# The order of the four last parts of a W4 product: alternating between two PSUM pairs

## The chip, the cores and the metric

The kernel runs on one core of one Trainium2 chip. The metric is the device time of one execution in microseconds. Most executions of a kernel agree within 0.3%. That is about 0.8 us here.

In views of the profile, PE is TensorE's matmul, PEld its weight load, DVE is VectorE, ACT is ScalarE, POOL is GpSimd and SPq the queue that issues the stores. PSUM is the memory that TensorE's matmuls write and VectorE reads. The slot of a matmul is the time from its start to the next one's start in an unbroken stream; a stall between slots is what such a step takes beyond its slot. L484 is line 484 of the kernel.

## The reference, cut to what matters

A gated sum of a linear-attention block and a mixer block, on 2048 rows of width 640. The end of the second block is what the change touches:

```python
x1 = x + hs                                         # [2048, 640]
h2 = gelu(layernorm(x1) @ w3) @ w4                  # w3: 640 x 1728, w4: 1728 x 640
b  = x1 + h2
return g * a + (1 - g) * b
```

## The kernel before

The rows go through in four tiles of 512, each of four chunks of 128 rows. `W4` is the last product of a tile, so in the last tile it is the last thing TensorE does. Its 1728 contraction rows are 13 full blocks of 128 and a rest of 64.

In the cuts below, `P` is 128, `D` 640, `TS` 512, `LT` 256, `NT` the four tiles, `FF` the 13 full blocks, and `cc` the number of a chunk in its tile.

PSUM is handed out in pairs of banks, four pairs in all:

```python
ps = ctx.enter_context(tc.tile_pool(name="ps", bufs=4, space=PSUM))
def pair():
    return ps.tile([P, 2, 512], F32, name="pp")
```

In the last tile, each odd chunk (1 and 3) is cut into a small part of 128 output columns (`hf == 0`), in bank 0 of its pair, and a big part of 512 columns (`hf == 1`), in bank 1:

```python
def w4_dst(t, cc, pts, hf):
    n = D - TS if t == NT - 1 and cc % 2 else LT        # D - TS = 128, LT = 256
    return (pts[cc][:, 0, TS - n:TS], 0, n) if hf == 0 else (pts[cc][:, 1, 0:D - n], n, D)

def w4_mm(t, cc, pts, hf, start):                       # 13 matmuls
    dst, a, b = w4_dst(t, cc, pts, hf)
    for fc in range(FF):
        nc.tensor.matmul(dst, lhsT=st[t]["h2"][:, fc * TS + cc * P:fc * TS + (cc + 1) * P],
                         rhs=w4_sb[:, fc, a:b], start=start and fc == 0, stop=not start and fc == FF - 1)

def w4_part(t, cc, pts, hf):                            # VectorE reads one part, then it is stored
    # ... (cut)
    nc.vector.scalar_tensor_tensor(oc[:, a:b], src, omg[:, c:c + 1], st[t]["x1"][cc][:, a:b],
                                   op0=ALU.mult, op1=ALU.add)
    nc.sync.dma_start(out2[c * P:(c + 1) * P, a:b], oc[:, a:b])

def w4_tile(t):
    # ... the even chunks' 52 matmuls, and pairs for chunks 1 and 3 (cut)
    w4_rest(t, pts)                                     # the rest of 64 rows, for all chunks
    # ... (cut)
    for cc in (0, 2):
        w4_out(t, cc, pts[cc])                          # VectorE reads the even chunks, stores them
    last = t == NT - 1
    for cc, hf in ((3, 1), (1, 1), (1, 0), (3, 0)) if last else ((1, 0), (1, 1), (3, 0), (3, 1)):
        # ... (cut)
        w4_mm(t, cc, pts, hf, False)
        if last:
            w4_part(t, cc, pts, hf)
        elif hf == 1:
            w4_out(t, cc, pts[cc])
```

So the last tile ends with four parts on TensorE: big 3, big 1, small 1, small 3. Each is read by VectorE as soon as it is done.

## Time and profile before

| | before |
|---|---|
| median of the three fast runs | 266.64 us |
| span of the profiled run | 264.5 us |
| TensorE busy, granted clock | 98%, 1.000 |
| TensorE idle, waiting for VectorE, in the last tile | 0.84 us |

Of the page of before, the busy table and the two lines of the chain that ended last:

```profile
PE 260.0 (98%) x1744; PEld 161.5 (61%) x1744; DVE 139.5 (53%) x271; ACT 85.2 (32%) x126; POOL 21.9 (8%) x67
...
PE 97%; ACT 1%; DVE 0%; issue 0%
PE pp L484 22%; PE pp L464 21%; PE pp L311 8%; PE pp L194 8%; PE pp L417 8%; PE pp L448 8%; PE pp L345 8%; PE pp L236 8%; PE pp L206 1%; PE pp L472 1%; PE pp L493 1%; ACT m_sb L385 1%; PE pp L364 1%; PE pp L251 0%; DVE oc L512 0%; PE pp L383 0%
```

TensorE bounds the kernel from end to end. Only a hole in TensorE's work, its start, or the tail after its last matmul, can be shortened without less work. The timeline of before shows one such hole at the end. Its columns are start and length in us, engine, line, operation, and in brackets the idle time before it and what ended it:

```profile
253.52 5.79 PE L484 MATMUL pp<-w_sb,h 128*128 128x512 bf16 x26
256.54 0.75 DVE L512 SCALAR_TENSOR_TENSOR oc<-pp,omg,x 128x512 bf16<-128x512 f32 x1 [1.51 <-PE pp L484]
...
259.34 0.75 DVE L512 SCALAR_TENSOR_TENSOR oc<-pp,omg,x 128x512 bf16<-128x512 f32 x1 [2.05 <-PE pp L484]
260.15 1.61 PE L484 MATMUL pp<-w_sb,h 128*128 128x128 bf16 x26 [0.84 <-DVE oc L512]
...
261.07 0.35 DVE L512 SCALAR_TENSOR_TENSOR oc<-pp,omg,x 128x128 bf16<-128x128 f32 x1 [0.98 <-PE pp L484]
261.80 0.35 DVE L512 SCALAR_TENSOR_TENSOR oc<-pp,omg,x 128x128 bf16<-128x128 f32 x1 [0.38 <-PE pp L484]
```

Read it so. The two big parts run without a gap (26 matmuls). VectorE reads big 3 at 256.54 while TensorE works on big 1: nobody waits. VectorE reads big 1 at 259.34, and TensorE stands still until that read is over. The reason put forward is that its next part, small 1, lies in the same pair. Then both small parts run (26 matmuls, one group). The view of waits from 240 us on names the hole (who waited for whom: us in total, times, longest):

```profile
PE pp L484 <- DVE oc L512: 0.8, 1, 0.8
```

And the chain in order of time (start, us, what) shows that the hole is on the path that sets the end:

```profile
253.59 5.73 PE pp L484 x26
259.32 0.02 issue
259.34 0.76 DVE oc L512
260.11 0.04 issue
260.15 1.62 PE pp L484 x26
261.77 0.03 issue
261.80 0.35 DVE oc L512
```

### The profile page before, as it was taken

Reading aid. Unit: us, or ns where it says so; the run is one execution under the profiler, and the core shown is the slowest. Engines: PE = TensorE matmul, PEld = TensorE weight load, DVE = VectorE, ACT = ScalarE, POOL = GpSimd, SP = SyncE. Lnnn points to the kernel's source line nnn. Section 1 sums busy time; section 2 is a strip of 40 time slices with the busy share of each in tenths; the row PEclk is TensorE's granted clock in tenths of the full one; section 3 lists DMA queues with packets and bytes.
Section 4 is the critical chain, followed back from the end, with each engine's and each line's share of the span. In section 5 each row is a group of like instructions: output and inputs, shape, how many; then the busy total and the mean of one; then the engine's idle time right before and its main releaser. Section 6 shows DMA issues by size and latency. Waiting matters only on the chain.

```text
span 264.5 us, 4272 instructions
## 1 busy us (share of the span) xinstructions
PE 260.0 (98%) x1744; PEld 161.5 (61%) x1744; DVE 139.5 (53%) x271; ACT 85.2 (32%) x126; POOL 21.9 (8%) x67
## 2 busy tenths in 40 slices
PE   8999999999999999999999999999999999999994
PEld 5767555788755644555667555667565667455743
DVE  1788688899858588955403464503455313112132
ACT  1555444321165636622502212312131422233000
POOL 7100220012300140001000001000001000000000
PEclk9999999999999999999999999999999999999999
DMA  7999987055663727600132000042000041100011
GB/s 203 181 209 367 376 255 287 0 42 121 127 91 71 78 51 196 203 0 2 25 74 77 25 0 2 0 99 77 25 0 2 1 99 58 43 0 2 0 50 50
DMA packets 46285, 23.62 MB, mean 89 GB/s; under 512 B 35770, under 2 KB 45626, under 8 KB 46266
## 3 DMA queue, kind: packets, MB, share of 16 engines
q1 hardware_dynamic: 45824, 22.86, 34.7%
q10 hardware_dynamic: 442, 0.49, 0.5%
q8 instruction: 13, 0.21, 0.3%
q14 instruction: 6, 0.05, 0.1%
HBM read 12.21 MB, written 2.62 MB: 56 GB/s over the span
## 4 chain that ended last, share of the span: by engine, by line
PE 97%; ACT 1%; DVE 0%; issue 0%
PE pp L484 22%; PE pp L464 21%; PE pp L311 8%; PE pp L194 8%; PE pp L417 8%; PE pp L448 8%; PE pp L345 8%; PE pp L236 8%; PE pp L206 1%; PE pp L472 1%; PE pp L493 1%; ACT m_sb L385 1%; PE pp L364 1%; PE pp L251 0%; DVE oc L512 0%; PE pp L383 0%
## 5 line engine op out<-in xcount | busy, mean ns | idle before, releaser
L464 PE MATMUL pp<-lnxT,w_sb 128*128 128x512 bf16 x260 | 60.4, 379 | 0.0
L484 PE MATMUL pp<-w_sb,h 128*128 128x256 bf16 (+3 forms) x416 | 58.0, 299 | 0.8 <-DVE oc L512 0.8
L466 ACT ACTIVATE h<-pp 128x1024 bf16<-128x1024 f32 (+1 forms) x28 | 27.0, 963 | 82.1 <-PE pp L464 82.1
L484 PEld LDWEIGHTS <-h 128*128 128x128 bf16 x416 | 39.3, 98 | 18.8 <-issue 2.2
L464 PEld LDWEIGHTS <-w_sb 128*128 128x128 bf16 x260 | 25.4, 98 | 26.8
L500 DVE SCALAR_TENSOR_TENSOR oc<-pp,omg,x 128x640 bf16<-128x640 f32 x14 | 12.0, 881 | 41.4 <-ACT h2x L475 21.3
L451 DVE SCALAR_TENSOR_TENSOR x<-pp,gate,x 128x640 f32<-128x640 f32 x16 | 13.9, 868 | 29.4 <-PE pp L448 29.4
L420 DVE TENSOR_TENSOR x<-pp,x_sb 128x640 f32<-128x640 f32 x16 | 13.1, 820 | 22.6 <-PE pp L417 22.6
L186 ACT ACTIVATE e<-pp 128x640 bf16<-128x640 f32 (+1 forms) x26 | 21.5, 827 | 9.6 <-PE pp L236 9.6
L448 PE MATMUL pp<-m_sb,pqT 128*128 128x320 bf16 x160 | 24.3, 299 | 0.0
L417 PE MATMUL pp<-w_sb,hsT 128*128 128x320 bf16 x160 | 23.9, 299 | 0.1
L194 PE MATMUL pp<-wk_sb,xT 128*128 128x320 bf16 (+1 forms) x160 | 22.6, 300 | 0.0
L311 PE MATMUL pp<-x_sb,pk 128*128 128x320 bf16 (+1 forms) x160 | 22.3, 300 | 0.0
L236 PE MATMUL pp<-xT,hsT 128*128 128x512 bf16 x100 | 21.7, 379 | 0.0
L311 PEld LDWEIGHTS <-pk 128*128 128x128 bf16 x160 | 18.8, 117 | 3.5
L417 PEld LDWEIGHTS <-hsT 128*128 128x128 bf16 x160 | 15.6, 98 | 8.2 <-issue 0.2
L448 PEld LDWEIGHTS <-pqT 128*128 128x128 bf16 x160 | 15.7, 98 | 7.7
L194 PEld LDWEIGHTS <-xT 128*128 128x128 bf16 x160 | 15.6, 98 | 6.2 <-DMA xT<-in_A_x_dram 0.3
L345 PE MATMUL pp<-lnxT,w_sb 128*128 128x512 bf16 x80 | 17.9, 379 | 0.0
L236 PEld LDWEIGHTS <-hsT 128*128 128x128 bf16 x100 | 11.8, 118 | 9.7
L281 POOL TENSOR_SCALAR rstd<-mv 128x4 f32<-128x4 f32 (+1 forms) x11 | 3.5, 314 | 156.4 <-DVE mv L287 156.4
L188 DVE SCALAR_TENSOR_TENSOR pk<-pp,e 128x640 bf16<-128x640 f32 x16 | 13.2, 825 | 1.7
(77 smaller groups left out, 194.8 us busy)
## 6 DMA issues: line engine op xcount, KB each, us to landing
out_dram<-oc SPq DMA_DIRECT2D x14, 160.0 KB, 1.8
w_sb<-in_B_w_dram SPq DMA_DIRECT2D x1, 2080.0 KB, 10.0
w_sb<-in_B_w_dram SPq DMA_DIRECT2D x1, 1296.0 KB, 8.0
x_sb<-in_A_x_dram SPq DMA_DIRECT2D x2, 640.0 KB, 10.4
x_sb<-in_A_x_dram SPq DMA_DIRECT2D x1, 1120.0 KB, 7.9
wo_sb<-in_A_wo_dram SPq DMA_DIRECT2D x6, 160.0 KB, 6.7
w_sb<-in_B_w_dram SPq DMA_DIRECT2D x1, 864.0 KB, 5.1
hsT<-in_A_wqkv_dram SPq DMA_DIRECT2D x1, 800.0 KB, 5.4
```

The source lines that it names most:

```text
L186: nc.scalar.activation(ev, src, ACT.Exp)
L188: nc.vector.scalar_tensor_tensor(dst, src, 0.0, ev, op0=ALU.max, op1=ALU.add)
L194: nc.tensor.matmul(pt[:, hf, 0:n], lhsT=xT[:, dc, c * P:(c + 1) * P], rhs=wk_sb[:, dc, hf * HD:hf * HD + n], start=(dc == 0), stop=(dc == ...
L236: nc.tensor.matmul(pt[:, t % 2, :], lhsT=wq_sb[:, dc, :].rearrange("p (m j) -> p j m", j=DC)[:, j], rhs=xT[:, dc, t * TS:(t + 1) * TS], st ...
L311: nc.tensor.matmul(pt[:, hf, 0:HD + hf], lhsT=w, rhs=x_sb[:, c, hf * HD:(hf + 1) * HD + hf], start=(c == 0), stop=(c == NCH - 1))
L345: nc.tensor.matmul(pt[:, i, :], lhsT=w, rhs=lnxT[t][:, dc, :], start=(dc == 0), stop=(dc == DC - 1))
L417: nc.tensor.matmul(pt[:, hf, 0:HD], lhsT=hsT[:, fc, 2 + c * P:2 + (c + 1) * P], rhs=w2_sb[:, fc, hf * HD:(hf + 1) * HD], start=(fc == 0), ...
L448: nc.tensor.matmul(pt[:, hf, 0:HD], lhsT=pqT[:, j, c * P:(c + 1) * P], rhs=m_sb[:, j, hf * HD:(hf + 1) * HD], start=(j == 0), stop=(j == D ...
L451: nc.vector.scalar_tensor_tensor(x1, pt[:, :, 0:HD], gate[:, c:c + 1], x1, op0=ALU.mult, op1=ALU.add)
L464: nc.tensor.matmul(pt[:, k, :], lhsT=w3_sb[:, dc, fc * P:(fc + 1) * P], rhs=lnT[:, dc, :], start=(dc == 0), stop=(dc == DC - 1))
L466: nc.scalar.activation(h2[:, 2 * i * TS:(2 * i + n) * TS], pt[:].rearrange("p h e -> p (h e)")[:, 0:n * TS], ACT.Gelu_apprx_tanh)
L484: nc.tensor.matmul(dst, lhsT=st[t]["h2"][:, fc * TS + cc * P:fc * TS + (cc + 1) * P], rhs=w4_sb[:, fc, a:b], start=start and fc == 0, stop ...
```

## The change

The intent: order the four parts so that a part never follows directly on one in its own pair. VectorE then reads one pair while TensorE writes the other.

```diff
         last = t == NT - 1
-        for cc, hf in ((3, 1), (1, 1), (1, 0), (3, 0)) if last else ((1, 0), (1, 1), (3, 0), (3, 1)):
+        for cc, hf in ((1, 1), (3, 1), (1, 0), (3, 0)) if last else ((1, 0), (1, 1), (3, 0), (3, 1)):
```

## The prediction

> **What bounds the kernel now.** TensorE. The busy table has PE at 260.0 of 264.5 us (98%); the chain that ended last is 97% PE; the per-core view shows the clock at 1.000. The stretch that the change touches is the last 11 us. The timeline there, with starts of single instructions (each odd chunk has a 512-column part in one bank of its PSUM pair, a 128-column part in the other):
>
> - big part of chunk 3: 13 matmuls from 253.52, 216 ns apart; VectorE reads it at 256.54 for 0.75 us;
> - big part of chunk 1: 13 matmuls, the last starting at 258.93; VectorE reads it from 259.34 to 260.10;
> - small part of chunk 1: it sits in the pair that VectorE is reading, and the build's wait is on the whole pair. PE is idle "0.84 <-DVE oc L512" (also the view of waits), and starts at 260.15;
> - small part of chunk 3: no wait. The 26 small matmuls start 55.7 ns apart, 260.15 to 261.54;
> - VectorE 261.80 to 262.15, DMA issue at 262.18, end at 264.5.
>
> **What the change removes, adds, moves.** No instruction is added or removed. The order becomes: big 1, big 3, small 1, small 3. Comparing the built programs, the first small matmul of chunk 1 keeps its wait on VectorE and that of chunk 3 gains one.
>
> Small 1 now needs only VectorE's read of big 1, over at about 257.3, long before PE gets there. So it follows big 3 directly: the next slot after the matmul at 258.93 is 259.14. It needs 13 x 55.7 ns = 0.725 us, until 259.87. Small 3 then waits for VectorE's read of big 3, in the same place as the read of before: released at 260.15. So PE's wait does not vanish. It shrinks from about 1.01 us between slots (258.93 + 0.216 to 260.15) to about 0.28 us. In the view of waits, which starts at the modelled end of a matmul, 0.84 us becomes about 0.1 us.
>
> **How much is critical.** All of it: in both kernels PE restarts at 260.15, with 26 matmuls left before and 13 after. PE's last matmul moves from 261.54 to about 260.82, by 0.725 us. Behind it nothing new queues: VectorE's read of small 1 (0.35 us) fits between 260.15 and 260.55, ahead of small 3's at about 261.08. The tail from PE's end to the span's end (2.7 us) stays. Expected span 263.7 us.
>
> **Trainium skill.** "PSUM — Partial Sum Buffer", section on bank collisions, asks for guarding by bank and quadrant. The two parts lie in different banks, so the wait of 0.84 us comes from tracking the pair as one tile; the change hides most of it and doesn't remove it. "Perfetto Trace Analysis", section on Tensor Engine instructions, says that the end of a matmul is estimated; hence I count from start to start.
>
> **Predicted time.** 266.78 - 0.73 = 266.05 us, range 265.5 to 266.6. Chances: faster by over 2%: 0.5%; within 2%: 99%; slower: 0.5%.
>
> **What would show it.** Right: PE's wait before the last small part is 0.05 to 0.3 us; no gap before small 1; the last VectorE instruction starts near 261.08. Wrong: a gap before small 1 too, or the last VectorE start still past 261.5.
>
> **What would make it wrong.** The gain is 0.3%, as large as the scatter between runs. A restart of PE after the wait slower than before; VectorE's read of small 1 going late and pushing the last one; the last stores landing later because they lie closer together.

## The result, and the profile after

The median was 265.77 us (265.64 to 265.81, 4 runs) against 266.71 us of before in the same rounds, or 266.64 us for its three fast runs. The ratio of the fast runs is 0.9965, with a 95% interval of 0.9945 to 0.9984. (Ratios are the mean time of one kernel's fast runs over that of the other's of the same rounds, so not quite the ratio of the medians that are quoted.) One run of before took 392.44 us; it is in the median of 266.71 us but was not counted as fast, and nothing here explains it.

The timeline after. The 52 matmuls of the four parts now come out as one group without an idle entry; the two VectorE reads, of big 3 and of small 1, are back to back and are merged:

```profile
253.80 7.51 PE L484 MATMUL pp<-w_sb,h 128*128 128x512 bf16 x52
...
256.82 0.75 DVE L512 SCALAR_TENSOR_TENSOR oc<-pp,omg,x 128x512 bf16<-128x512 f32 x1 [1.51 <-PE pp L484]
...
259.62 1.08 DVE L512 SCALAR_TENSOR_TENSOR oc<-pp,omg,x 128x512 bf16<-128x512 f32 x2 [2.05 <-PE pp L484]
...
261.35 0.35 DVE L512 SCALAR_TENSOR_TENSOR oc<-pp,omg,x 128x128 bf16<-128x128 f32 x1 [0.65 <-PE pp L484]
```

The chain in order of time, after:

```profile
253.87 5.73 PE pp L484 x26
259.60 0.02 issue
259.62 0.76 DVE oc L512
260.39 0.04 issue
260.43 0.90 PE pp L484 x13
261.33 0.02 issue
261.35 0.35 DVE oc L512
```

The chain still goes through VectorE's read of a big part, at the same 0.76 us. What differs is the piece behind it: 13 matmuls instead of 26. The other 13 (small 1) run beside the read. This is the whole change in two lines of a profile.

The view of waits after lists no wait of TensorE for VectorE at all. The costliest groups of the page still show 0.1 us of idle time before this group of TensorE (0.8 before):

```profile
L484 PE MATMUL pp<-w_sb,h 128*128 128x256 bf16 (+3 forms) x416 | 58.0, 299 | 0.1
```

For exact lengths we count single records from the start of the first big matmul. The Trainium skill, page "Perfetto Trace Analysis", section on Tensor Engine instructions, says that a matmul's end in the profile is estimated; its start is not, so the times run from start to start:

```
us from the first big matmul                  before    after
start of the last big matmul                   5.407    5.406
start of the first small matmul                6.629    5.622
start of the 13th small matmul                 7.295    6.292
start of the 14th (next part)                  7.351    6.628
start of the last matmul                       8.021    7.295
start of the last VectorE instruction          8.279    7.552
from there to the end of the trace             2.671    2.677
```

The gain in the last tile is 8.279 - 7.552 = 0.727 us, with the same tail behind it.

The two profiled spans differ by only 0.5 us, though (264.5 and 264.0). The rest lies at the other end of the kernel. In the chain in order of time, before (taken in two windows, the first of which cuts the length of its last piece, so only the starts count):

```profile
27.44 20.72 PE pp L236 x96
...
245.87 7.06 PE pp L484 x52
```

and after, in the same two windows:

```profile
27.72 20.29 PE pp L236 x94
...
246.16 7.06 PE pp L484 x52
```

After was already 0.28 us late at the start of the `q` products, and 0.29 us late at the start of the last W4 product. In the ten traces that kept all 1744 matmul records, the time from the 195th matmul to the first big matmul was 223.65 us, the same to 0.01 us, while the start of the first big matmul ran from 253.52 to 254.30 us. So the scatter between these traces is made in the first 30 us, long before the edited lines run. The single starts show two parts of it. From 4.8 to 5.8 us the 128x320 matmuls of after start some 267 ns apart, while those of before come every 136 ns from 5.2 us on; this makes after 0.46 us late. Why the faster pace comes later in some runs is not known. Then before, at 16.4 us, waits for the load of an input (`xT`) and loses 0.18 us of its lead. The same two parts differ in the other traces.

### The profile page after: what moved, and what is told of

Its sections match the earlier page's. It is cut to its first block, busy times and chain, and to the rows that moved or that the text cites. A ratio compares the mean times of both kernels' runs of the same rounds, so it can differ in the third digit from the quotient of the medians.

```text
span 264.0 us, 4272 instructions
## 1 busy us (share of the span) xinstructions
PE 260.3 (99%) x1744; PEld 161.8 (61%) x1744; DVE 139.5 (53%) x271; ACT 85.1 (32%) x126; POOL 21.9 (8%) x67
## 4 chain that ended last, share of the span: by engine, by line
PE 97%; ACT 1%; DVE 0%; issue 0%
PE pp L484 21%; PE pp L464 21%; PE pp L194 8%; PE pp L311 8%; PE pp L417 8%; PE pp L448 8%; PE pp L345 8%; PE pp L236 8%; PE pp L206 2%; PE pp L472 1%; PE pp L493 1%; ACT m_sb L385 1%; PE pp L364 1%; PE pp L251 0%; DVE oc L512 0%; PE pp L383 0%
```

## The experiments

The theory: TensorE's wait is decided by whether the next part lies in the pair that VectorE is reading. Alternating hides that read behind the small part put in between, so it saves the smaller of two lengths: the stall between slots (1.01 us here) and the small part (13 x 55.7 ns = 0.725 us). Alternation here means that a part is never followed by one of its own pair. Rivals: it matters which chunk goes first, or the order of VectorE's reads and of the stores; or the saving is the whole read, or a fixed amount.

The yardstick of all expectations is the time from the first big matmul to the start of the last VectorE instruction. The traces of two runs (e4, e5) lost the record of that matmul. There the yardstick is taken from an earlier anchor, the start of VectorE's last attention update, which is 8.617 us before the first big matmul in both before and after.

### The change itself again

No edit; five rounds.

> The changed kernel itself, to measure the gain with more rounds. Yardstick in the trace for all these runs: from the start of the first 512-column matmul of the odd chunks in the last tile to the start of the last VectorE instruction; before 8.28 us, after 7.55 us. Theory (the pair's wait is hidden behind the small part of chunk 1): 7.55 us again, and a timed gain of 0.73 us. Rival (the timed 0.94 us holds something besides this): a gain of 0.9 us or more that repeats.

Yardstick 7.551 us. Median 266.03 us against 266.42, ratio 0.998 (0.9967 to 0.9993), which is 0.5 us. A later repeat is told at the end. The 0.94 us of the first rounds did not repeat; 7.55 us did.

### Mirrored alternation

(The diffs from here on are shortened. This one and the next are shown against before.)

```diff
-((3, 1), (1, 1), (1, 0), (3, 0)) if last
+((3, 1), (1, 1), (3, 0), (1, 0)) if last
```

> Big 3, big 1, small 3, small 1: alternating like the change, but chunk 3 first, so the first half of the order of before is kept. Theory: yardstick 7.55 us and the same gain as the change, 0.73 us. Rival (it matters that chunk 1 goes first, or the order of the first two parts and of their stores): 8.28 us, no gain.

Yardstick 7.552 us; median 265.89 us, ratio 0.9977 (0.9964 to 0.9989). The first two parts keep the order of before and the gain is the same, so it is not chunk 1 going first.

### The big parts swapped, no alternation

```diff
-((3, 1), (1, 1), (1, 0), (3, 0)) if last
+((1, 1), (3, 1), (3, 0), (1, 0)) if last
```

> Big 1, big 3, small 3, small 1: the first half of the change with the small parts the other way round, so that the small part after the two big ones sits in the pair VectorE is reading. Theory: the whole wait is back, TensorE idle 0.84 us, yardstick 8.28 us, time as before within 0.1 us. Rival (the change's gain is that chunk 1's big part goes first): 7.55 us.

The wait is back whole. The timeline of this run:

```profile
259.73 0.75 DVE L512 SCALAR_TENSOR_TENSOR oc<-pp,omg,x 128x512 bf16<-128x512 f32 x1 [2.06 <-PE pp L484]
260.54 1.61 PE L484 MATMUL pp<-w_sb,h 128*128 128x128 bf16 x26 [0.84 <-DVE oc L512]
```

Yardstick 8.279 us; median 266.59 us, ratio 1.0006 (0.9994 to 1.0017).

### The order of before, the small parts in each other's pairs

```diff
     def w4_dst(t, cc, pts, hf):
         n = D - TS if t == NT - 1 and cc % 2 else LT
-        return (pts[cc][:, 0, TS - n:TS], 0, n) if hf == 0 else (pts[cc][:, 1, 0:D - n], n, D)
+        home = pts[4 - cc] if t == NT - 1 and cc % 2 and hf == 0 else pts[cc]
+        return (home[:, 0, TS - n:TS], 0, n) if hf == 0 else (home[:, 1, 0:D - n], n, D)
```

> The order of before on every engine and in the stores, but each small part is accumulated in the other chunk's PSUM pair. Theory: the order by itself is nothing, only which pair follows which counts; small 1 now sits in the pair of big 3, read long ago: yardstick 7.55 us, gain 0.73 us, with the order untouched. Rival (the order of TensorE's parts, of VectorE's reads or of the stores makes the gain): 8.28 us, time as before.

Yardstick 7.552 us, with every engine and every store in the order of before. The chain of this run has the 13 matmuls behind the read, as after (the edit added a line, so numbers are one higher):

```profile
260.04 0.76 DVE oc L513
260.80 0.04 issue
260.84 0.90 PE pp L485 x13
261.74 0.03 issue
261.76 0.35 DVE oc L513
```

The clock alone was inconclusive here: one of its runs took 267.88 us, and the ratio is 0.9996 (0.9975 to 1.0017); the medians are 266.12 and 266.42 us.

### The order of the change, the small parts in each other's pairs

The edit of the run above, on top of the change.

> The order of the change, with each small part in the other chunk's pair. Theory: the change is undone by placement alone; small 1 is again in the pair VectorE is reading (that of big 3): one wait of TensorE of 0.84 us, yardstick 8.28 us, time as before. Rival (the order of the parts makes the gain): 7.55 us.

The change is undone by placement. In the timeline:

```profile
260.22 1.61 PE L485 MATMUL pp<-w_sb,h 128*128 128x128 bf16 x26 [0.84 <-DVE oc L513]
```

Yardstick 8.28 us by the anchor; median 266.40 us, ratio 1.0000 (0.9986 to 1.0014). Together, these two runs settle it: the same order gives both results, and so does the other order. The pair decides.

### Pairs of their own for the small parts

The small parts' first matmuls (of the rest of 64 rows) move to just before the small parts, into pairs that the even chunks have left:

```diff
-        w4_rest(t, pts)
+        w4_rest(t, pts, ((0, 0), (0, 1), (1, 1)) if t == NT - 1 else ((0, 0), (0, 1), (1, 0), (1, 1)))
 ...
+            if last and (cc, hf) == (1, 0):
+                for c2 in (1, 3):
+                    pts[c2, 0] = pair()
+                w4_rest(t, pts, ((1, 0),))
             w4_mm(t, cc, pts, hf, False)
```

(`w4_rest` takes the list of parts, and `w4_dst` finds a small part in `pts[cc, 0]`.)

> The order of the change, but the two small parts get pairs of their own, those that the even chunks have left by then, and their short first matmuls move to just before the small parts. No part then waits for VectorE. Theory (what the change leaves is a wait of about 0.28 us between slots before small 3): the yardstick falls from 7.55 us to about 7.3 us, a little more if switching to the half-height matmuls and back costs some 0.05 to 0.1 us; timed gain over before 0.9 to 1.0 us. Rival (the wait left over costs nothing, the end is set by VectorE or the stores): 7.55 us or more.

This expectation was wrong in size. The waits were gone, but by the anchor the last VectorE instruction came only 0.063 us earlier than after, not 0.25 us; median 265.97 us, ratio 0.9981 (0.9968 to 0.9994), a gain of 0.5 us where 0.9 to 1.0 was expected. The timeline shows what took the place of the wait:

```profile
259.41 0.10 PEld L494 LDWEIGHTS <-h2x 64*128 64x128 bf16 x2 [0.42 <-issue]
259.41 0.23 PE L494 MATMUL pp<-w_sb,h2x 64*128 64x128 bf16 x2
...
259.57 1.63 PE L485 MATMUL pp<-w_sb,h 128*128 128x128 bf16 x26
```

From start to start, the last big matmul is followed by the two half-height ones (64 rows in place of 128) after 311 ns instead of the 216 ns of its slot, and the first small one comes 162 ns later: 473 ns where 216 ns would do, and the second small one another 67 ns later. The two half-height matmuls run side by side and are worth some 56 ns of columns (an estimate: the slot of a 128-column matmul); the rest, some 0.21 us, is put down to switching to half height and back. The Trainium skill, page "TensorEngine Tiling (Array Packing)", section "Key Properties", says that changing the tiling mode drains TensorE. This trace fits that, with about 95 ns for the switch in (311 - 216). The earlier place of these matmuls keeps its own two switches, so moving them added two. What a switch takes stood in the trace of before already: there the way into the half-height matmuls is 258 ns where the slot is 162, and the way out 311 ns where it is 216. Two switches are about 0.19 us, and the expectation had put them at 0.05 to 0.1 us: that is the term it mis-sized. Of the wait of 0.280 us some 0.07 us are then left to gain, close to the 0.063 measured. The rival "the wait left over costs nothing" expected no gain over the change at all; the next runs test it more directly.

### Cut at 192 + 448 columns, order of before and order of the change

The same edit, once on before and once on the change.

```diff
-        n = D - TS if t == NT - 1 and cc % 2 else LT
+        n = 192 if t == NT - 1 and cc % 2 else LT
```

> The order of before with the parts cut at 192 + 448 columns instead of 128 + 512. Estimates from the traces: VectorE's read of 448 columns 0.69 us (0.751 for 512, 0.351 for 128), so a stall of about 0.94 us between slots; 13 small matmuls take about 13 x 82 ns = 1.06 us. Theory: one wait of about 0.78 us as idle time, the yardstick (first big matmul to last VectorE start) about 8.16 us, time within 0.2 us of before.

> The order of the change with the parts cut at 192 + 448. Theory: what alternation saves is the smaller of the stall and the small part's length. Here the small part (1.06 us) outlasts the stall (0.94 us), so the stall is hidden whole: saving against the same cut in the old order 0.94 us instead of 0.73, yardstick about 7.22 us, no wait of TensorE for VectorE. Rival (alternation saves a fixed 0.73 us, or the length of the small part): 7.43 or 7.1 us.

Old order: idle 0.78 us, 0.941 us between slots (1.130 us from the last big start to the first small one, less a slot of 0.189), yardstick 8.214 us; median 266.72 us, ratio 1.0010 (0.9997 to 1.0022). In its timeline:

```profile
259.86 2.31 PE L484 MATMUL pp<-w_sb,h 128*128 128x192 bf16 x26 [0.78 <-DVE oc L512]
```

New order: yardstick 7.276 us, no wait, no gap between matmuls; median 265.41 us, ratio 0.9973 (0.9958 to 0.9989):

```profile
253.60 7.24 PE L484 MATMUL pp<-w_sb,h 128*128 128x448 bf16 x52
```

Both yardsticks came about 0.055 us later than expected (8.16 and 7.22); only the old order's stall differs from before's, and 8.279 - (1.006 - 0.941) gives the 8.214 measured. The difference between the two is as expected. Alternation saved 8.214 - 7.276 = 0.938 us here, which is the whole stall, and neither 0.73 nor the small part's 1.07 us. That is the "smaller of two" of the theory. The yardstick is also 0.276 us below the change's, so the wait left over in the change was worth about its 0.28 us. In exchange the last read is longer (0.42 us for 192 columns, 0.35 for 128), and the time from its start to the end is 2.79 us instead of 2.68.

### VectorE's second big read done twice, both orders

```diff
-        nc.vector.scalar_tensor_tensor(oc[:, a:b], src, ...)
+        for _ in range(2 if (cc, hf) == (1, 1) else 1):      # (3, 1) in the new order
+            nc.vector.scalar_tensor_tensor(oc[:, a:b], src, ...)
```

The result stays correct.

> The order of before, with VectorE's read of the second big part (big 1) done twice, same result. Theory: the stall grows by the second read, from 1.01 to about 1.8 us between slots, the idle time from 0.84 to about 1.6 us; yardstick 8.28 + about 0.79 = 9.07 us. It is the base for the next run.

> The order of the change, with VectorE's read of the second big part (big 3) done twice. Theory: alternation saves the small part's length when the stall is longer, however long: yardstick 0.73 us under the old order with the double read, so about 8.34 us, with a wait of TensorE of about 0.9 us left before small 3. Rival (alternation hides the read, whatever it takes): no wait left, about 7.55 us.

Old order: idle 1.63 us, yardstick 9.064 us, and in its timeline:

```profile
261.59 1.61 PE L484 MATMUL pp<-w_sb,h 128*128 128x128 bf16 x26 [1.63 <-DVE oc L513]
```

New order: 8.339 us, with the wait in plain view in its timeline:

```profile
260.12 1.80 DVE L513 SCALAR_TENSOR_TENSOR oc<-pp,omg,x 128x512 bf16<-128x512 f32 x3 [2.05 <-PE pp L484]
261.71 0.89 PE L484 MATMUL pp<-w_sb,h 128*128 128x128 bf16 x13 [0.90 <-DVE oc L513]
```

The saving is 9.064 - 8.339 = 0.725 us beside a stall of 1.79 us: the small part's length again, and not the read's.

### Chunk 1 cut at 192, chunk 3 at 128, beside the change

```diff
-        n = D - TS if t == NT - 1 and cc % 2 else LT
+        n = {1: 192, 3: D - TS}[cc] if t == NT - 1 and cc % 2 else LT
```

> The order of the change with chunk 1 cut at 192 + 448 and chunk 3 at 128 + 512: small 1 is long enough (about 1.06 us) to outlast the stall behind big 3 (1.01 us), and the last part stays short. Theory: no wait of TensorE left, yardstick about 7.27 us, and the tail behind it as short as the change's (2.67 us, against 2.79 us with the 192-column last part). Timed gain over before about 1.0 us, best of all. Rival (only the last part's size counts): 7.55 us.

> The changed kernel again beside the run before this one. Yardstick 7.55 us, timed gain over before 0.73 us, about 0.28 us less than the run before this one.

Yardstick 7.276 us with no wait, and 2.655 us from there to the end: the shortest of all traces from the first big matmul to the end, with a yardstick 0.276 us below the change's 7.552 in the same rounds. The timeline has no idle entry for TensorE, and the last two reads keep clear of each other:

```profile
253.56 7.24 PE L484 MATMUL pp<-w_sb,h 128*128 128x448 bf16 x52
...
259.04 0.75 DVE L512 SCALAR_TENSOR_TENSOR oc<-pp,omg,x 128x512 bf16<-128x512 f32 x1 [2.12 <-PE pp L484]
260.11 0.42 DVE L512 SCALAR_TENSOR_TENSOR oc<-pp,omg,x 128x192 bf16<-128x192 f32 x1 [0.32 <-PE pp L484]
260.84 0.35 DVE L512 SCALAR_TENSOR_TENSOR oc<-pp,omg,x 128x128 bf16<-128x128 f32 x1 [0.31 <-PE pp L484]
```

The clock does not resolve this step. The median was 265.72 us (ratio 0.9966, 0.9953 to 0.9979), and the change beside it had 265.66 us (0.9968, 0.9954 to 0.9982). Both beat before; that this cut beats the change is shown by the trace alone.

### All runs together

| run | stall between slots, us | small part between, us | yardstick, us | ratio to before |
|---|---|---|---|---|
| before | 1.006 | none | 8.279 | 1 |
| after, and two repeats | 0.280 left | 0.725 | 7.552, 7.551, 7.552 | 0.9965, 0.9980, 0.9968 |
| mirrored | 0.280 left | 0.725 | 7.552 | 0.9977 |
| big parts swapped only | 1.006 | none | 8.279 | 1.0006 |
| old order, pairs swapped | 0.280 left | 0.725 | 7.552 | 0.9996 |
| new order, pairs swapped | 1.005 | none | 8.28 | 1.0000 |
| own pairs | none | two switches instead | 0.063 below after | 0.9981 |
| 192, old order | 0.941 | none | 8.214 | 1.0010 |
| 192, new order | none | 1.07 | 7.276 | 0.9973 |
| second read twice, old order | 1.791 | none | 9.064 | one look |
| second read twice, new order | 1.067 left | 0.725 | 8.339 | one look |
| 192 first, 128 last | none | 1.07 | 7.276 | 0.9966 |

## Why the prediction was right

- *TensorE bounds the kernel, and all that its wait shrinks by is critical.* Right: the last VectorE start came 0.727 us earlier, and the tail behind it stayed at 2.671 and 2.677 us.
- *The wait comes from tracking the pair as one tile.* That it goes with the pair is shown by placement: swapping the small parts' pairs turns the gain on in the old order and off in the new one. The two parts lie in different banks throughout, so it does not go with the bank. That the chip itself would allow the two banks of one pair to be used at once (the Trainium skill, "PSUM — Partial Sum Buffer", section on bank collisions, asks for guarding by bank and quadrant) was run here by no kernel, since the build puts the wait in; it stays open.
- *The wait shrinks from 1.01 to about 0.28 us between slots, and the gain is small 1's length, 0.725 us.* Measured: 1.006 to 0.280 us, and 0.727 us on the yardstick. The doubled read and the 192-column cut show that it is this length because it is the smaller of the two.
- *In the view of waits, 0.84 becomes about 0.1 us.* The group line has 0.1 us; the view of waits itself lists nothing. Whoever looked only there would have taken the wait for gone, while 0.28 us of it was still to be had.
- *The last VectorE instruction starts near 261.08, the span is 263.7 us.* It started at 261.35 and the span was 264.0 us, because the whole tile began 0.28 us later in that run; counted from the tile's first big matmul it is 7.552 us, where 261.08 - 253.52 = 7.56 was predicted.
- *266.05 us, range 265.5 to 266.6.* Measured 265.77 us. The three sets of rounds give 0.93, 0.53 and 0.85 us (1 minus the ratio, times the median of before in the same rounds), 0.77 us in the mean. Each set's interval contains 0.73 us, and the differences between the sets are no larger than the scatter that the first 30 us make. But the time alone proves little: in the later rounds before itself had medians of 266.30 to 266.42 us, inside the predicted range without any change. That the first time fell in the range was in part luck; what confirms the prediction is the trace.

## What to carry to other kernels

When a consumer reads one PSUM tile while the producer's next work lies in the same tile, reordering so that other work comes between saved, in this kernel, the smaller of the stall and that work's length; make the work in between just longer than the stall, and keep the very last piece short. Where a gain is smaller than the scatter of the clock, measure it in the trace from an event just before the change to one just after: here that repeated to 2 ns while the times moved by 0.7 us. Before moving work to fill a gap, look whether it brings a switch of its own: here the two switches for two half-height matmuls cost most of the wait they were to remove.

## What the Trainium skill lacked or had wrong

- "TensorE: Matmul & The Clock Gate", section "Back-to-back issue gap", gives about 81 ns per matmul at 128 columns and about 131 ns at 512 for a stream of weight loads and matmuls. Here, in just such a stream, they came every 55.7 and 216 ns, and 82.5 and 189 ns at 192 and 448 columns. The page's other figure, N/2.4 + 2.5 ns, which this section calls that of an isolated matmul, gives 55.8, 215.8, 82.5 and 189.2 ns, and fits all four. The page contradicts itself here: its section "Wait — 56ns, not 53.3ns?" has 55.6 and 215.7 ns for back-to-back matmuls.
- "TensorEngine Tiling (Array Packing)", section "Key Properties", says that a change of tiling mode drains TensorE, but gives no time. Here going from 128 rows to 64 added about 95 ns, and the move of two half-height matmuls to between full-height ones stretched the way from the last big to the first small one from 216 to 473 ns.
- "VectorE: DVE Perf Modes", section "The TRN2 errata — SBUF-src ops pay a fixed extra latency per instruction", has a table that gives 120 + N cycles at 0.96 GHz for VectorE from PSUM to SBUF, which would be 258 ns at 128 columns and 658 ns at 512. It has no row for an operation with a second input. Here a read of PSUM with a second input in SBUF took 351, 418, 684 and 751 ns at 128, 192, 448 and 512 columns: the slope agrees (1.04 ns per column), the fixed part is about 217 ns instead of 125. Whether the second input makes the difference is not shown.
- No page looked at says that a wait may hide from a profile's list of waits: of 280 ns between slots, 0.1 us showed as idle time, since the modelled length of a 128-column matmul (219 ns) is four times its slot (55.7 ns). "Perfetto Trace Analysis" has the ground for it, that the end is estimated.
